# Moving the second half of the MLP's second product ahead of the second part of its first product

## The chip, the cores and the metric

The kernel runs on one core of a Trainium2 chip. The metric is the device time of one execution in microseconds. The kernel before took 2911.58 us, the median of three runs (2907.26 to 2915.17).

## The reference

Two stages follow one another. The first is a spectral layer over eight sequences of 3008 tokens and 256 channels; the second is an MLP over all 24064 tokens.

```python
X = np.fft.rfft(x, axis=1)
Yr = Xr @ w_r - Xi @ w_i + b_r
Yi = Xr @ w_i + Xi @ w_r + b_i
Yr = np.sign(Yr) * np.maximum(np.abs(Yr) - 0.01, 0.0)      # the same for Yi
x = np.fft.irfft(Yr + 1j * Yi, n=3008, axis=1)             # (8 * 3008, 256)
h = x @ w_in                                               # 256 -> 2048
g = np.maximum(0.01 * h, h)
out = g @ w_out                                            # 2048 -> 256
```

## The kernel before, in words

**Spectral part.** The transform of 3008 = 47 x 64 points is done in two stages of matmuls with constant matrices, per batch: `fwd` (fold, the transform over 47, `stage_a`), then `mid` (`stage_b`, the transform over 64; `proj`, the products with `w_r` and `w_i` and the soft threshold; `stage_g`, the way back over 64), then `inverse` (the way back over 47, at L480). Between these stages the data goes through DRAM (`u_dram`, `v_dram`). Their matmuls write PSUM banks of the tag `psf`, of which there are two. They are recorded at L78 (a helper that multiplies pairs), L343 and L480.

**MLP part.** The tokens are cut into 47 chunks of 512. In each chunk the 2048 hidden channels are cut into 8 groups of 256, so there are 47 x 8 = 376 steps `(ci, q)`. Every number is held as a high and a low part in fp32r, and a product is three matmuls (high by high, high by low, low by high).

For a step the first product (256 hidden channels by 512 tokens, over 256 channels) is cut into 2 x 2 blocks and made with seven block products instead of eight. `forms` (L496) makes the seven combinations of the tokens, `yh` and `yl`, once per chunk; those of the weights are made at the start.

- `moe_a` (L532, called part A here): four of the seven products, twelve matmuls of 256 columns at L92, into two PSUM banks `b1` and `b2` of the tag `psh` (four banks, so two steps). Then what was made is taken out: ACT copies the first half of `b1` (`p1`, L542), DVE adds the second half to it (`u2`, L543) and makes one of the four blocks of `g` (L545, L546).
- `moe_b` (L549, part B): the other three products, nine matmuls at L92, into the halves of the same two banks. So B's first product may only write once L542 and L543 have read, and its second once L546 has. Then ACT and DVE make the rest of `g`: the leaky ReLU of one block (L556), the sum of two blocks (L557), the leaky ReLU of three blocks (L559), the rounding to the high part `gh` (L561) and the low part `gl` (L563). `gf`, `gh` and `gl` have two buffers each.
- `moe_o` (L566, called with `eh` 0 or 1; parts O0 and O1): the second product for one half of the 256 output channels, two blocks of 128 hidden channels, six matmuls of 512 columns at L576, added up over the chunk's eight steps in a bank of the tag `pso`. It is that of two steps before (`LAG = 2`). After the chunk's last step ACT copies the bank (L581) and SP sends it out (L582).

**What sets the order.** `in_order` ties the matmuls of each part to the last matmul of the part before, in issue order only, so the parts' order on TensorE is that in which `moe` (L607) calls them:

```python
in_order(moe_a, ci, q)
if i >= LAG: in_order(moe_o, *steps[i - LAG], 0)
next(nxt, None); yield ...
in_order(moe_b, ci, q)
if i >= LAG: in_order(moe_o, *steps[i - LAG], 1)
next(nxt, None); ...; yield ...
```

At each `next(nxt, None)` a piece of the next chunk's `inverse` and `forms` is written down, at each `yield` a piece of the next batch's `fwd` and `mid`, as far as their shares are due. These are not tied: the framework's planner (`schedule_with_timeline_sim=True`) runs a timeline of its own over the whole program and puts each engine's instructions in the order in which they come to be ready there. The order so found is fixed in the program; on the chip each engine follows it and waits on semaphores.

Of the kernel before, what the change touches and what calls it, by code (L numbers as in the profile page):

```python
# [30 lines left out]
def spectral_mlp_kernel(  # L31
# [52 lines left out]
    def in_order(part, *args):  # L84

        with tc.issue_after(mlp[0].ins) if mlp else nullcontext():
            part(*args)
# [505 lines left out]
    def tokens(ci):  # L593

        yield
        for p in due[ci]:
            v_load(p)
            yield
        for _ in range(4 - len(due[ci])):
            yield  # L600
        for eh in range(NH):
            for p in due[ci]:
                inverse(p, eh)
                yield
        yield from forms(ci)

    def moe():  # L607

        for i, (ci, q) in enumerate(steps):
            if q == 0:  # L610
                nxt = tokens(ci + 1) if ci + 1 < nch else iter(())
            in_order(moe_a, ci, q)
            if i >= LAG:
                in_order(moe_o, *steps[i - LAG], 0)
            next(nxt, None)
            yield ci + (q + 0.5) / NQ
            in_order(moe_b, ci, q)
            if i >= LAG:
                in_order(moe_o, *steps[i - LAG], 1)
            next(nxt, None)  # L620
            if q == NQ - 1:
                for _ in nxt:
                    pass
            yield ci + (q + 1) / NQ
        for s in steps[-LAG:]:
            for eh in range(NH):
                in_order(moe_o, *s, eh)
# [92 lines left out]
    for i, pos in enumerate(moe()):  # L720
        if i % 2 == 0 and len(converted) < NQ:
            with tc.issue_after(made[0].ins):
                next(wout, None)
        if i in (2, 4):
            with tc.issue_after(parted[0].ins), tc.issue_after(parted[1].ins):
                next(fp.gen)
        while cur + 1 < NB - 1 and pos >= (read[cur + 1] if cur >= 0 else 0):
            for s in streams:
                s.finish()
            cur += 1  # L730
            streams = ([Stream(fwd(cur + 1), FWD + 4 * CS)] if cur else []) + [mids[cur]]
        frac = (pos - read[cur]) / (read[cur + 1] - read[cur]) if cur + 1 < NB else 1
        if cur == 0:
            frac = max(0, frac - 0.2) * 1.25
        work = frac / 0.95 * sum(s.total for s in streams)
        with tc.issue_after(converted[-1].ins) if cur == 0 else nullcontext():
            for s in streams:
                s.to(work / s.total)
                work = max(0, work - s.total)
# [103 lines left out]
```

## Time and profile before

| | |
|---|---|
| median of 3 runs | 2911.58 us (2907.26 to 2915.17) |
| the profiled execution | 2913.01 us, span 2911.2 us |
| TensorE (PE) busy | 2685.1 us, 92% of the span |
| VectorE (DVE) busy | 1896.7 us, 65% |
| ScalarE (ACT) busy | 1671.0 us, 57% |
| GpSimd (POOL) busy | 241.1 us, 8% |
| mean granted TensorE clock | 0.982 |
| first matmul of the MLP | 129.8 us after the start |

The times of rows are microseconds from the span's start and durations in microseconds; in groups the columns are the count, the busy time in us with the mean of one in ns, and the engine's idle time just before them in us with what ended it. PE rows are matmuls; their ends are modelled, and one starts while the one before still runs, so the distance from start to start says more than the duration. DVE and ACT rows are the instructions that read and write PSUM and SBUF.

### The profile page before, as it was taken

To read this page: it belongs to the slowest core of one execution; us is meant where nothing else is said; L and a number is where in the kernel's file an instruction comes from. 1 tells how busy PE (TensorE), PEld (TensorE's weight loads), DVE (VectorE), ACT (ScalarE), POOL (GpSimd) and SP (SyncE) were. 2 spreads that over 40 slices of the span, in tenths; PEclk is the share of its full clock that TensorE was granted. 3 is DMA by queue.
4 is the path that set the end of the run, shared out by engine and by line. 5 is a ranking of instruction groups with operands and counts; after the bars stand their busy time and mean duration, and the time that the engine had idled before them with its cause. 6 is when DMAs were issued, how large, how long until landed. Compare 5 with 4: busy or idle time off the path is not lost.

```text
span 2911.2 us, 43056 instructions
## 1 busy us (share of the span) xinstructions
PE 2685.1 (92%) x16300; PEld 2313.2 (79%) x16300; DVE 1896.7 (65%) x3403; ACT 1671.0 (57%) x3174; POOL 241.1 (8%) x180
## 2 busy tenths in 40 slices
PE   5989989999899999999999999999999999999988
PEld 4678878888788887888878887788887888777777
DVE  6676766666666666666666666666666766555554
ACT  4756645656565664566546665566655766454544
POOL 0001120001200012000110001100011000000000
PEclk8999999999999999999999999999999999999999
DMA  8521132111321113111222111221122111000000
GB/s 242 161 71 47 44 96 58 43 44 33 96 64 33 44 35 91 54 54 33 55 79 60 44 33 53 81 63 44 29 65 83 54 44 29 29 29 15 15 8 15
DMA packets 119916, 165.16 MB, mean 57 GB/s; under 512 B 13601, under 2 KB 69917, under 8 KB 119709
## 3 DMA queue, kind: packets, MB, share of 16 engines
q1 hardware_dynamic: 79120, 115.55, 13.0%
q10 hardware_dynamic: 40589, 46.87, 6.3%
q8 instruction: 128, 2.10, 0.3%
q14 instruction: 79, 0.65, 0.1%
HBM read 86.60 MB, written 75.76 MB: 56 GB/s over the span
## 4 chain that ended last, share of the span: by engine, by line
PE 43%; DVE 27%; ACT 18%; issue 4%; POOL 1%; DMA 1%; DVEq 0%; ACTq 0%; POOLq 0%; SPq 0%
PE psh L92 18%; PE pso L576 16%; DVE gl L563 7%; PE psf L78 7%; ACT gh L561 6%; ACT gf L559 5%; DVE gf L557 4%; DVE gf L545 3%; DVE gf L546 3%; DVE u L543 2%; PE psf L480 2%; PE psf L343 2%; ACT zf L400 1%; ACT zf L396 1%; DVE yl L506 1%
## 5 line engine op out<-in xcount | busy, mean ns | idle before, releaser
L92 PE MATMUL psh<-yh,win_hi 128*128 128x256 f32 x2632 | 792.3, 301 | 124.6 <-DVE gf L546 84.0
L563 DVE TENSOR_TENSOR gl<-gf,gh 128x1024 fp32r<-128x1024 f32 x376 | 466.1, 1240 | 448.7 <-ACT gh L561 444.4
L92 PE MATMUL psh<-yl,win_hi 128*128 128x256 f32 x2632 | 741.6, 282 | 0.1
L92 PE MATMUL psh<-yh,win_lo 128*128 128x256 f32 x2632 | 740.0, 281 | 0.0
L92 PEld LDWEIGHTS psh<-yh,win_hi 128*128 128x128 f32 x2632 | 500.4, 190 | 246.8 <-DVE gf L546 129.0
L576 PE MATMUL pso<-gh,wout_lo 128*128 128x512 f32 x1504 | 598.1, 398 | 0.0
L576 PE MATMUL pso<-gh,wout_hi 128*128 128x512 f32 x1504 | 598.0, 398 | 0.0
L576 PE MATMUL pso<-gl,wout_hi 128*128 128x512 f32 x1504 | 595.7, 396 | 0.0
L559 ACT ACTIVATE gf<-gf 128x768 f32<-128x768 f32 x376 | 318.3, 846 | 447.9 <-DVE gf L557 440.0
L92 PEld LDWEIGHTS psh<-yl,win_hi 128*128 128x128 f32 x2632 | 501.2, 190 | 23.3 <-DVE yl L506 0.3
L92 PEld LDWEIGHTS psh<-yh,win_lo 128*128 128x128 f32 x2632 | 500.1, 190 | 0.1
L561 ACT CAST gh<-gf 128x1024 fp32r<-128x1024 f32 x376 | 395.0, 1051 | 9.4 <-PE pso L576 3.2
L557 DVE TENSOR_TENSOR gf<-psh,u 128x512 f32<-128x512 f32 x376 | 258.4, 687 | 206.1 <-PE psh L92 205.7
L576 PEld LDWEIGHTS pso<-gl,wout_hi 128*128 128x128 f32 x1504 | 286.4, 190 | 65.6 <-DVE wout_lo L202 0.2
L576 PEld LDWEIGHTS pso<-gh,wout_hi 128*128 128x128 f32 x1504 | 287.0, 191 | 35.5 <-issue 0.2
L576 PEld LDWEIGHTS pso<-gh,wout_lo 128*128 128x128 f32 x1504 | 286.4, 190 | 32.1
L556 ACT ACTIVATE gf<-psh 128x256 f32<-128x256 f32 x376 | 145.2, 386 | 269.2 <-PE psh L92 248.6
L379 POOL TENSOR_TENSOR kb<-bias,kc 128x512 f32<-128x512 f32 x84 | 127.3, 1515 | 1714.0 <-ACT kc L376 1624.7
L543 DVE TENSOR_TENSOR u<-psh,p 128x256 f32<-128x256 f32 x376 | 157.1, 418 | 93.4 <-ACT p L542 93.3
L545 DVE TENSOR_TENSOR gf<-psh,u 128x256 f32<-128x256 f32 x376 | 158.7, 422 | 28.9 <-PE psf L78 0.5
L546 DVE TENSOR_TENSOR gf<-psh,gf 128x256 f32<-128x256 f32 x376 | 157.8, 420 | 6.1
L542 ACT COPY p<-psh 128x256 f32<-128x256 f32 x376 | 137.2, 365 | 16.2 <-PE psh L92 14.6
(134 smaller groups left out, 3274.7 us busy)
## 6 DMA issues: line engine op xcount, KB each, us to landing
u<-u_dram SPq DMA_DIRECT2D x192, 128.0 KB, 2.7
v_dram<-v ACTq DMA_DIRECT2D x192, 128.0 KB, 2.4
out_dram<-ob SPq DMA_DIRECT2D x94, 256.0 KB, 2.0
vin<-v_dram SPq DMA_DIRECT2D x96, 240.0 KB, 3.4
xin<-x_dram SPq DMA_DIRECT2D x90, 240.0 KB, 3.0
u_dram<-xin ACTq DMA_DIRECT2D x72, 240.0 KB, 2.4
u_dram<-xin SPq DMA_DIRECT2D x24, 240.0 KB, 4.0
raw<-w_out_dram SPq DMA_DIRECT2D x8, 512.0 KB, 5.1
```

What stands on the lines that cost most here:

```text
L78: last = nc.tensor.matmul(dst, a, b, start=(i == 0), stop=(i == len(terms) - 1))
L92: mlp[:] = [nc.tensor.matmul(dst, a, b, start=start and i == 0, stop=i == 2, skip_group_check=True)]
L542: act.copy(p1, b1[:, lo])
L543: dve.tensor_add(u2, b1[:, hi], p1)
L545: dve.tensor_add(g[:, 3], b2[:, hi], u2)
L546: dve.tensor_add(g[:, 3], b2[:, lo], g[:, 3])
L556: act.activation(g[:, 0], b1[:, lo], AF.Prelu, alpha=SLOPE)
L557: dve.tensor_add(g[:, 1:3], b2.rearrange("p (k n) -> p k n", k=2), u2.unsqueeze(1).broadcast_to([P, 2, HT]))
L559: act.activation(g[:, 1:4], g[:, 1:4], AF.Prelu, alpha=SLOPE)
L561: cp = act.copy(gh, g)
L563: parted[:] = [cp, dve.tensor_sub(gl, g, gh.bitcast(F32))]
L576: mlp[:] = [nc.tensor.matmul(po, a[:, f, s], r[:, i], start=(f == 0 and j == 0), stop=(f == NF - 1 and j == 2),)]
```

## The change

In `moe` the call of O1 goes from behind B to ahead of it. A step's order on TensorE was A, O0, B, O1; it is A, O0, O1, B. The piece of the next chunk (`next`) and the `yield` that stand between O0 and B now stand between O0 and O1. No instruction is added, removed or resized; the last `LAG` steps' O parts after the loop stay as they were.

```diff
@@ -614,9 +614,9 @@
                 in_order(moe_o, *steps[i - LAG], 0)
             next(nxt, None)
             yield ci + (q + 0.5) / NQ
-            in_order(moe_b, ci, q)
             if i >= LAG:
                 in_order(moe_o, *steps[i - LAG], 1)
+            in_order(moe_b, ci, q)
             next(nxt, None)
             if q == NQ - 1:
                 for _ in nxt:
```

## The prediction

> **What bounds the kernel now.** I read the first page for the shares, then the groups by line for what TensorE (PE) waits for, then the timeline of one step in the last chunks, where hardly any spectral work is left.
>
> ```profile
> span 2911.2 us, 43056 instructions
> PE 2685.1 (92%) x16300; PEld 2313.2 (79%) x16300; DVE 1896.7 (65%) x3403; ACT 1671.0 (57%) x3174; POOL 241.1 (8%) x180
> ```
> ```profile
> L92 PE MATMUL psh<-yh,win_hi 128*128 128x256 f32 x2632 | 792.3, 301 | 124.6 <-DVE gf L546 84.0 <-DVE u L543 39.3
> L576 PE MATMUL pso<-gh,wout_hi 128*128 128x512 f32 x1504 | 598.0, 398 | 0.0
> L78 PE MATMUL psf<-wr_hi,eh 128*128 128x256 f32 x336 | 79.4, 293 | 28.5 <-ACT eh L358 16.2 <-DVE yc L512 8.2 <-DVE eh L359 2.1
> L78 PE MATMUL psf<-xz,fa_hi 120*120 120x512 f32 (+1 forms) x168 | 62.9, 414 | 20.0 <-DVE xz L254 11.5 <-DVE xz L255 6.8 <-ACT gf L556 1.1
> L78 PE MATMUL psf<-zh,gb_hi 128*128 128x512 f32 x168 | 61.7, 426 | 9.8 <-ACT zh L407 5.8 <-ACT kc L376 3.2 <-DVE zh L408 0.2
> L480 PE MATMUL psf<-ga,vin 120*128 120x128 f32 x832 | 110.6, 276 | 2.4 <-DVE y L486 1.2 <-ACT v L418 0.3 <-ACT xin L264 0.3
> L343 PE MATMUL psf<-fb,u 128*128 128x128 f32 x672 | 89.0, 275 | 3.7 <-DMA u<-u_dram 1.8 <-ACT ob L581 0.9 <-ACT yc L493 0.6
> ```
> ```profile
> 0.00:130.00 130.00, 96.88 (x382) 65.82 (x383) 84.85 (x147) 77.80 (x151) 0.82 (x6) 0.88 0.71 209
> ```
>
> PE is the fullest engine. Its idle time is 2911.2 - 2685.1 = 226.1 us, and 124.6 us of it stand before the first matmul of an L92 product, nearly all for L546 and L543: the two vector instructions that empty the first product part's banks before the second part may write them. The first 130 us (set-up) hold 33.1 us of the idle time, so in the MLP stretch 124.6 of 193 us, 65%, is this one wait. Now one step of the last chunks, PE, then ACT, then DVE.
>
> ```profile
> 2823.72 0.39 PE L92 MATMUL psh<-yh,win_hi 128*128 128x256 f32 x1 [0.37 <-DVE gf L546]
> ...
> 2824.41 0.29 PE L92 MATMUL psh<-yh,win_lo 128*128 128x256 f32 x1
> 2824.54 0.39 PE L576 MATMUL pso<-gh,wout_hi 128*128 128x512 f32 x1
> 2824.77 0.40 PE L576 MATMUL pso<-gh,wout_lo 128*128 128x512 f32 x1
> 2825.93 0.28 PE L92 MATMUL psh<-yh,win_hi 128*128 128x256 f32 x1
> 2826.17 0.28 PE L92 MATMUL psh<-yh,win_lo 128*128 128x256 f32 x1
> 2826.28 0.28 PE L92 MATMUL psh<-yh,win_hi 128*128 128x256 f32 x1
> 2827.22 0.28 PE L92 MATMUL psh<-yh,win_lo 128*128 128x256 f32 x1
> 2827.34 0.40 PE L576 MATMUL pso<-gh,wout_hi 128*128 128x512 f32 x1
> 2828.48 0.39 PE L576 MATMUL pso<-gl,wout_hi 128*128 128x512 f32 x1
> 2829.05 0.38 PE L92 MATMUL psh<-yh,win_hi 128*128 128x256 f32 x1 [0.18 <-DVE u L543]
> 2830.03 0.38 PE L92 MATMUL psh<-yh,win_hi 128*128 128x256 f32 x1 [0.37 <-DVE gf L546]
> ```
> ```profile
> 2825.47 0.85 ACT L559 ACTIVATE gf<-gf 128x768 f32<-128x768 f32 x1 [1.70 <-DVE gf L557]
> 2826.35 1.05 ACT L561 CAST gh<-gf 128x1024 fp32r<-128x1024 f32 x1
> 2827.30 0.36 ACT L542 COPY p<-psh 128x256 f32<-128x256 f32 x1
> ```
> ```profile
> 2824.74 0.69 DVE L557 TENSOR_TENSOR gf<-psh,u 128x512 f32<-128x512 f32 x1 [1.08 <-PE psh L92]
> 2827.43 1.22 DVE L563 TENSOR_TENSOR gl<-gf,gh 128x1024 fp32r<-128x1024 f32 x1 [2.00 <-ACT gh L561]
> 2828.57 0.42 DVE L543 TENSOR_TENSOR u<-psh,p 128x256 f32<-128x256 f32 x1
> 2829.55 0.42 DVE L546 TENSOR_TENSOR gf<-psh,gf 128x256 f32<-128x256 f32 x1
> ```
>
> Call the parts A (first product, four products of three matmuls), B (three products) and O0, O1 (six matmuls each). Matmuls start 0.117 us apart at 256 columns (2826.17 to 2826.28 and the like) and 0.231 at 512 (2824.54 to 2824.77). The step repeats every 2830.03 - 2823.72 = 6.31 us, while its 21 + 12 matmuls need 21 x 0.117 + 12 x 0.231 = 5.23. The loop that takes 6.31 is not on PE: B's last matmul (2824.41) releases L557, then L559, L561, L563 follow one on the other; p of the next A, though its product was done at 2826.17 + 0.28 = 2826.45, runs behind L561 at 2827.30; u runs behind L563 at 2828.57; L546 ends at 2829.97 and lets B go on at 2830.03.
>
> **The floor.** For all matmuls at these distances: 376 steps x 5.23 = 1966 us. Spectral ones: the six groups of wr, wn, wd (336 with the high, 168 with the low part each), 1512 x 0.117 = 177; fa 252, of which by their two shapes 216 x 0.231 and 36 x 0.117 = 54; gb 252 x 0.231 = 58; ga and fb 1504 x 0.112 (estimate from eight of them in a row, below) = 168. With the 130 us ahead: 130 + 1966 + 457 = 2553 us. So PE starts are late by 358 us, more than the idle column shows, because a matmul's modelled end covers some of each gap. By the same 65%, 231 us belong to B's waits, 127 to spectral waits and ends.
>
> [...]
>
> **The change part by part.** Nothing is added or removed. Six matmuls a step, O1, go ahead of B. In the last step of a chunk's products the L581 copy and the output DMA of the second half go with them.
>
> Cover of A's emptying: PE runs O0 between A and B today, 6 x 0.231 = 1.39 us; afterwards O0 and O1, 2.77. Working the new step from the start of B's last matmul (t = 0) with the durations of the rows above: A follows at once, its four products are done at 0.63, 0.98, 1.33 and 1.68 (0.117 a start, 0.28 for the last one). L557 runs from 0.33 to 1.02; until then ACT has nothing, so p, which needs the first product only, fits in from 0.7 to 1.06, before L559. u runs from 1.1 to 1.5, L545 (0.42, the same shape) to 1.95, L546 to 2.4. PE reaches B at 0.12 + 12 x 0.117 + 2.77 = 4.3, so there are 1.9 us to spare. L563, not ready before 1.1 + 0.85 + 1.05 = 3.0, no longer gets between: the 1.22 us that stood before u come after L546. If p goes behind L559 instead, L546 ends at 3.3 to 3.6 and 0.7 us are still to spare. Gain where no spectral work is: 6.31 - 5.23 = 1.08 us a step.
>
> What is left of B's waits (231 us): lower end 0; upper end, if the emptying comes no sooner after A than now, what of each wait exceeds the added 1.39 us:
>
> ```profile
> PE psh L92 <- DVE gf L546: 84.0, 166, 3.2
> PE psf L78 <- ACT eh L358: 16.2, 10, 2.5
> ```
>
> In the first row (us in total, times, longest) the mean is 0.5 us and the longest wait 3.2, so about a third of the sum can stay, 70 us (an estimate). I take 35, nearer to none, since L563 is out of the way.
>
> The 127 us of spectral waits: from 0 to 127. Spectral matmuls keep the place ahead of B, but PE comes there with its queue full, so their inputs have had longer; on the other hand a step is shorter by 0.9. About half: 60.
>
> ```profile
> L581 ACT COPY ob<-pso 128x512 f32<-128x512 f32 x94 | 54.3, 577 | 58.5 <-PE pso L576 58.5
> ```
>
> Costed at nothing: O1's earlier place (gh and gl of two steps before were finished a step ago; the two buffers of each are read before B instead of after, so L561 finds them free sooner); the moved copies, 47 of the 94 in this row (ACT, which runs them, is 57% busy), and their 47 output DMAs on SP, which are now issued about one B ahead of where they were, before the loads that the planner's next steps put there; ACT and SP are behind PE here, as the row's 58.5 us of waiting for O shows, and cover gone, the copies would cost 47 x 0.58 = 27 us. At the end O0 of the last step has only the previous step's O parts ahead of it and waits some 1.2 us for L563.
>
> Sum: 2553 + 35 + 60 = 2648 of span. The profiled execution took 2913.0, 1.8 more than its span and 1.4 more than the median of 2911.6: 2650. Own range 2555 (nothing left) to 2752 (70 + 127).
>
> **Rivals.** *The emptying keeps its place.* The planner may leave p behind L561 and u behind L563. Then the loop from B's last matmul to the next B is what it was, and only O1 has changed sides: no change, 2912. Against it: in the step shown L561 began at 2826.35, 0.10 us before p's product was done, so the order there is that of readiness, and in the new step p is ready before L559. [...]
>
> *Spectral work falls behind.* Today a step has two openings for it, before B and between B's first two products:
>
> ```profile
> 1206.57 0.39 PE L78 MATMUL psf<-zh,gb_lo 128*128 128x512 f32 x1
> 1207.04 0.27 PE L92 MATMUL psh<-yh,win_lo 128*128 128x256 f32 x1
> 1207.15 0.28 PE L78 MATMUL psf<-wn_hi,eh 128*128 128x256 f32 x1
> 1208.45 0.28 PE L78 MATMUL psf<-wd_hi,eh 128*128 128x256 f32 x1
> 1213.44 1.05 PE L343 MATMUL psf<-fb,u 128*128 128x128 f32 x8
> ```
>
> With B ready early, both come at once, so a chain PE - ACT/DVE - PE gets one round a step. Needed: 672/8 = 84 frequency pairs at two rounds, 84 forward halves at one, 832/8 = 104 inverse halves two to a round: 304, against 312 steps before the last eight chunks. If a round takes 1.3 steps, 83 steps are missing; five are in hand, since the forms for a chunk are done long before it starts:
>
> ```profile
> 1490.25 0.68 DVE L506 TENSOR_TENSOR yl<-yc,yh 128x512 fp32r<-128x512 f32 x1
> 1527.30 0.28 PE L92 MATMUL psh<-yh,win_hi 128*128 128x256 f32 x1
> ```
>
> The other 78 would run with PE drained, each at up to the longest wait for such an input today, 2.5 us (the L358 row above): 195 us in place of the 60: 2785.
>
> *Slower.* If each of today's stretches needs a step of its own and nothing drains: the PE rows have 402 stretches of spectral matmuls, 145 of them inside B as shown; without the last chunks' about 380. With a step of 6.5 us (5.23 + 457/376, rounded up) and 5.35 in the last 64: 130 + 380 x 6.5 + 64 x 5.35 + 2 = 2944. It decides from about 376 such rounds on, where the same sum passes 2913. Against it: many stretches are two pieces of one round, and some steps have none.
>
> **How the numbers follow.** Forecast 0.65; spectral work behind 0.20; emptying in place 0.06; slower 0.07; something between, 0.02. A measurement of this kernel can tell about 0.3% from no change. Faster: 0.65 + 0.20 + the between and a part of the third: 0.89; same 0.04; slower 0.07. The range takes in most of the second case and of the forecast's own range: 2575 to 2800.
>
> **What would show it.** On ACT p ahead of L561, on DVE u and L546 ahead of L563; the L92 idle column from 124.6 to below 40; steps of 5.3 us in the last chunks and about 6.5 in the middle; POOL, DVE and ACT busy times unchanged. Wrong if PE waits at the first product of a chunk for L505/L506 (spectral work behind), if p still follows L561, or if the psf groups' idle time grows.

## The result and the profile after

The changed kernel takes 2604.09 us (median of 4 runs, 2600.34 to 2604.30) against 2909.90 (4 runs): a ratio of 0.8944, 95% interval 0.8928 to 0.8960. The prediction was 2650, with 2575 to 2800 as its range: faster, as forecast, and by 46 us more than forecast.

The first page and the PE groups of the profile after, in the columns used before:

```profile
span 2598.6 us, 42643 instructions
PE 2537.5 (98%) x16300; PEld 2281.5 (88%) x16300; DVE 1897.1 (73%) x3403; ACT 1668.5 (64%) x3174; POOL 229.6 (9%) x180
...
L92 PE MATMUL psh<-yh,win_hi 128*128 128x256 f32 x2632 | 752.3, 286 | 13.8 <-DVE gf L546 10.6 <-DVE u L543 3.0
L92 PE MATMUL psh<-yl,win_hi 128*128 128x256 f32 x2632 | 738.3, 280 | 0.6 <-DVE yl L506 0.5
...
L343 PE MATMUL psf<-fb,u 128*128 128x128 f32 x672 | 93.9, 275 | 9.6 <-DMA u<-u_dram 9.6
L78 PE MATMUL psf<-wr_hi,eh 128*128 128x256 f32 x336 | 77.9, 285 | 1.9 <-ACT eh L358 1.8
L78 PE MATMUL psf<-xz,fa_hi 120*120 120x512 f32 (+1 forms) x168 | 58.9, 380 | 0.0
L78 PE MATMUL psf<-zh,gb_hi 128*128 128x512 f32 x168 | 56.6, 396 | 0.0
```

ACT and DVE do the same work in the same time (DVE 1896.7 and 1897.1 us, ACT 1671.0 and 1668.5). What is gone is PE's waiting: 124.6 us before the products at L92 are 13.8, and the spectral groups, which waited 28.5, 20.0, 9.8 and 3.7 us, now wait 1.9, 0, 0 and 9.6. One of the last steps after, PE, then ACT, then DVE:

```profile
2525.17 0.28 PE L92 MATMUL psh<-yh,win_lo 128*128 128x256 f32 x1
2525.28 0.28 PE L92 MATMUL psh<-yh,win_hi 128*128 128x256 f32 x1
...
2525.87 0.28 PE L92 MATMUL psh<-yh,win_lo 128*128 128x256 f32 x1
...
2526.68 0.39 PE L576 MATMUL pso<-gh,wout_hi 128*128 128x512 f32 x1
...
2529.45 0.28 PE L92 MATMUL psh<-yh,win_hi 128*128 128x256 f32 x1
```
```profile
2526.18 0.37 ACT L542 COPY p<-psh 128x256 f32<-128x256 f32 x1 [1.27 <-PE psh L92]
2526.45 0.85 ACT L559 ACTIVATE gf<-gf 128x768 f32<-128x768 f32 x1
2527.34 1.06 ACT L561 CAST gh<-gf 128x1024 fp32r<-128x1024 f32 x1
```
```profile
2525.48 0.69 DVE L557 TENSOR_TENSOR gf<-psh,u 128x512 f32<-128x512 f32 x1
2526.59 0.42 DVE L543 TENSOR_TENSOR u<-psh,p 128x256 f32<-128x256 f32 x1 [0.41 <-ACT p L542]
2527.58 0.42 DVE L546 TENSOR_TENSOR gf<-psh,gf 128x256 f32<-128x256 f32 x1
2528.42 1.23 DVE L563 TENSOR_TENSOR gl<-gf,gh 128x1024 fp32r<-128x1024 f32 x1 [0.42 <-ACT gh L561]
```

B's last matmul starts at 2525.17, A at 2525.28. p now runs ahead of L559 and L561, u and L546 ahead of L563. L546 ends at 2528.00; B starts at 2529.45, and PE does not stop for it. Where the 312.6 us of span went, by stages (the view of busy time by stretch; columns: the stretch, its length, then busy time and count of PE, weight loads, DVE, ACT and POOL, granted clock, DMA), after and then before. The middle rows are the first 320 steps, the last rows the 56 steps that have little or no spectral work, with the end:

```profile
0.00:124.00 124.00, 93.25 (x381) 64.30 (x381) 84.62 (x147) 77.63 (x150) 0.82 (x6) 0.90 0.73 219
124.00:2286.50 2162.50, 2136.47 (x13971) 1940.59 (x13971) 1606.42 (x2903) 1416.94 (x2726) 228.73 (x174) 1.00 0.22 61
2286.50:2598.60 312.10, 307.74 (x1953) 276.59 (x1952) 206.02 (x354) 173.93 (x299) 0.00 (x0) 1.00 0.06 19
```
```profile
129.80:2537.50 2407.70, 2251.45 (x13972) 1968.82 (x13971) 1610.34 (x2904) 1420.43 (x2727) 240.27 (x174) 0.99 0.19 55
2537.50:2911.20 373.70, 336.94 (x1953) 278.79 (x1951) 201.51 (x352) 172.97 (x298) 0.00 (x0) 1.00 0.05 16
```

The middle gave 245.2 us, the last steps 61.6 (1.1 a step, the 1.08 of the prediction's clean step), the set-up 5.8.

### The profile page after: what moved, and what is told of

It reads as the page before. It is cut to its first block, busy times and chain, and to the rows that moved or that the text cites. A ratio compares the mean times of both kernels' runs of the same rounds, so it can differ in the third digit from the quotient of the medians.

```text
span 2598.6 us, 42643 instructions
## 1 busy us (share of the span) xinstructions
PE 2537.5 (98%) x16300; PEld 2281.5 (88%) x16300; DVE 1897.1 (73%) x3403; ACT 1668.5 (64%) x3174; POOL 229.6 (9%) x180
## 4 chain that ended last, share of the span: by engine, by line
PE 89%; DVE 3%; DMA 2%; ACT 1%; issue 0%; ACTq 0%; SPq 0%; DVEq 0%
PE pso L576 38%; PE psh L92 34%; PE psf L78 11%; PE psf L480 3%; PE psf L343 3%; DMA u<-u_dram 1%; DMA u_dram<-xin 1%; DVE yl L506 0%; DVE gl L563 0%; DMA raw<-w_out_dram 0%; DVE gf L557 0%; ACT gh L561 0%; DVE yt L511 0%; ACT gf L559 0%; DVE yc L512 0%
## 5 line engine op out<-in xcount | busy, mean ns | idle before, releaser
L92 PE MATMUL psh<-yh,win_hi 128*128 128x256 f32 x2632 | 752.3, 286 | 13.8 <-DVE gf L546 10.6
L92 PE MATMUL psh<-yl,win_hi 128*128 128x256 f32 x2632 | 738.3, 280 | 0.6 <-DVE yl L506 0.5
L92 PE MATMUL psh<-yh,win_lo 128*128 128x256 f32 x2632 | 737.9, 280 | 0.0
L576 PE MATMUL pso<-gh,wout_hi 128*128 128x512 f32 x1504 | 593.9, 395 | 0.0
L576 PE MATMUL pso<-gl,wout_hi 128*128 128x512 f32 x1504 | 591.1, 393 | 0.5 <-DVE gl L563 0.5
L576 PE MATMUL pso<-gh,wout_lo 128*128 128x512 f32 x1504 | 590.4, 393 | 0.0
L563 DVE TENSOR_TENSOR gl<-gf,gh 128x1024 fp32r<-128x1024 f32 x376 | 471.8, 1255 | 92.7 <-ACT gh L561 90.6
L92 PEld LDWEIGHTS psh<-yh,win_hi 128*128 128x128 f32 x2632 | 497.0, 189 | 30.7 <-DVE gf L546 15.4
L92 PEld LDWEIGHTS psh<-yl,win_hi 128*128 128x128 f32 x2632 | 497.0, 189 | 12.5 <-DVE yl L506 1.0
L92 PEld LDWEIGHTS psh<-yh,win_lo 128*128 128x128 f32 x2632 | 496.6, 189 | 0.2
L557 DVE TENSOR_TENSOR gf<-psh,u 128x512 f32<-128x512 f32 x376 | 259.1, 689 | 256.3 <-PE psh L92 255.1
L561 ACT CAST gh<-gf 128x1024 fp32r<-128x1024 f32 x376 | 396.4, 1054 | 7.1
L559 ACT ACTIVATE gf<-gf 128x768 f32<-128x768 f32 x376 | 320.0, 851 | 49.5 <-DVE gf L557 47.7
L576 PEld LDWEIGHTS pso<-gl,wout_hi 128*128 128x128 f32 x1504 | 282.5, 188 | 62.9 <-DVE gl L563 1.0
L576 PEld LDWEIGHTS pso<-gh,wout_hi 128*128 128x128 f32 x1504 | 283.1, 188 | 46.9 <-ACT gh L561 0.4
L576 PEld LDWEIGHTS pso<-gh,wout_lo 128*128 128x128 f32 x1504 | 282.9, 188 | 44.9
L379 POOL TENSOR_TENSOR kb<-bias,kc 128x512 f32<-128x512 f32 x84 | 119.0, 1417 | 1530.6 <-ACT kc L376 1409.6
L545 DVE TENSOR_TENSOR gf<-psh,u 128x256 f32<-128x256 f32 x376 | 159.3, 424 | 29.7 <-PE psh L92 2.0
L546 DVE TENSOR_TENSOR gf<-psh,gf 128x256 f32<-128x256 f32 x376 | 159.1, 423 | 9.0
```

What stands on the lines that cost most here:

```text
L92: mlp[:] = [nc.tensor.matmul(dst, a, b, start=start and i == 0, stop=i == 2, skip_group_check=True)]
L545: dve.tensor_add(g[:, 3], b2[:, hi], u2)
L546: dve.tensor_add(g[:, 3], b2[:, lo], g[:, 3])
L557: dve.tensor_add(g[:, 1:3], b2.rearrange("p (k n) -> p k n", k=2), u2.unsqueeze(1).broadcast_to([P, 2, HT]))
L559: act.activation(g[:, 1:4], g[:, 1:4], AF.Prelu, alpha=SLOPE)
L561: cp = act.copy(gh, g)
```

## The experiments

Two theories could explain such a gain. **Loop**: the limit was the loop B - L557 - L559 - gh (L561) - gl (L563) - u - L546 - B; the change breaks it because A is done sooner, so that the planner puts the emptying of A's banks (p, u, L545, L546) ahead of gh and gl in ACT's and DVE's queues. **Cover**: what counts is that PE has 1.39 us more work between A and B. The experiments set the two apart: the order on PE and the order in the queues are changed one without the other. All ratios are against the kernel before on the same chip (2907 to 2910 us). The diffs are shortened, and the comments in them are added. Where lines are added to a kernel, the line numbers below `moe_a` move by a few in its rows.

### The queue order alone (e1_late_cast)

```diff
+    def moe_c(ci, q, after=None):            # the end of moe_b, called one step later
+        g = cast_t.pop((ci, q))
...
+        with tc.issue_after(after[0].ins) ...: cp = act.copy(gh, g)              # behind p (L542)
...
+        with tc.issue_after(after[1].ins) ...: dve.tensor_sub(gl, g, gh...)      # behind L546
...
             in_order(moe_a, ci, q)
+            if i: moe_c(*steps[i - 1], emptied.pop((ci, q)))
```

> TensorE order of the kernel before (A, O0, B, O1), so the cover between A and B stays 1.39 us; only the queues differ: the cast to gh is issued behind the next step's p on ACT and gl behind the next step's L546 add on DVE. Loop theory (the limit was the loop B - L557 - L559 - gh - gl - u - L546 - B, broken when A's emptying goes ahead of gh and gl): from B's last matmul at 0, A starts at 1.5, p runs 2.05 to 2.4, the last add ends at 3.75, and PE gets to B at 4.3, so the wait is gone: steps of 5.3 to 5.5 us in the last chunks, total 2600 to 2690. Cover theory (what counts is the 1.39 us of matmuls more between A and B): no cover added, no gain: steps of 6.3 us, total 2880 to 2915.

2627.31 us, ratio 0.9036 (0.9022 to 0.9049); a step at the end, where there is no spectral work, takes 5.23 us (6.39 before; here and below the mean of the steps 370 to 373). On ACT and DVE the emptying is ahead of gh and gl in all 375 steps. The L92 row:

```profile
L92 PE MATMUL psh<-yh,win_hi 128*128 128x256 f32 x2632 | 756.1, 287 | 25.5 <-DVE gf L546 17.8 <-DVE u L543 7.0
```

With the order of the parts on PE untouched (the planner moved spectral matmuls among them), 281 of the 306 us come. The cover is not the main cause; whether it adds something is asked with e6.

### The cover without the queue order (e2_behind, e8_before_behind)

```diff
-        act.copy(p1, b1[:, lo])
-        dve.tensor_add(u2, b1[:, hi], p1)
+        with tc.issue_after(parted[0].ins) ...: act.copy(p1, b1[:, lo])              # behind gh
+        with tc.issue_after(parted[1].ins) ...: dve.tensor_add(u2, b1[:, hi], p1)    # behind gl
```

e2 makes this edit in the changed kernel, e8 in the kernel before.

> TensorE order of the changed kernel (A, O0, O1, B) with its 2.77 us of cover, but p is issued behind the gh cast of the step before and u behind its gl. Loop theory: gl ends at 4.2, u at 4.7, the last add at 5.5 after B's last matmul, PE is at B at 4.3, so the step is again 6.3 us in the last chunks and the total 2870 to 2930. Cover theory: the cover is what helps, total 2600 to 2690.

> The kernel before (A, O0, B, O1) with p behind the gh cast and u behind gl in all steps, where its planner does so in 240 of 375: the partner of e2, same queues, 1.39 us less cover. Loop theory: the loop does not go through O1, so the time is that of e2, 3000 to 3070. Cover theory: 1.39 us less cover in 376 steps should cost some 300 us against e2: 3250 to 3350.

e2: 3034.08 us, 1.0428 (1.0411 to 1.0446). e8: 3017.73 us, 1.0379 (1.0358 to 1.0400). A late step of e2, PE, ACT and DVE (there gh is L563, gl L565, u L545, the last add L548):

```profile
2991.94 0.28 PE L92 MATMUL psh<-yh,win_lo 128*128 128x256 f32 x1
2992.05 0.40 PE L578 MATMUL pso<-gh,wout_hi 128*128 128x512 f32 x1
...
2995.15 0.39 PE L92 MATMUL psh<-yh,win_hi 128*128 128x256 f32 x1 [0.20 <-DVE u L545]
...
2996.14 0.39 PE L92 MATMUL psh<-yh,win_hi 128*128 128x256 f32 x1 [0.37 <-DVE gf L548]
```
```profile
2992.45 1.05 ACT L563 CAST gh<-gf 128x1024 fp32r<-128x1024 f32 x1
2993.41 0.36 ACT L543 COPY p<-psh 128x256 f32<-128x256 f32 x1
```
```profile
2993.53 1.23 DVE L565 TENSOR_TENSOR gl<-gf,gh 128x1024 fp32r<-128x1024 f32 x1 [1.99 <-ACT gh L563]
2994.68 0.42 DVE L545 TENSOR_TENSOR u<-psh,p 128x256 f32<-128x256 f32 x1
2995.66 0.42 DVE L548 TENSOR_TENSOR gf<-psh,gf 128x256 f32<-128x256 f32 x1
```

A was done at 2992.2, p ran at 2993.41, u at 2994.68: with all the cover of the change, the step is 6.30 us again. With the queues fixed this way the 1.39 us are worth nothing (e2 is 16 us slower than e8). Both are above my 2870 to 2930 for e2, because I had equated them with the kernel before: its planner had put p ahead of gh in 135 of 375 steps, the edit in none, and that alone costs 110 us (e8). The late step was right, 6.30 us. e8, whose expectation followed e2's result, is in its range.

### Part of the cover, and none (e4_three, e5_no_cover, e7_nocover_late)

e4 moves three of O1's six matmuls; e5 and e7 call A, B, O0, O1, and e7 has e1's late cast besides.

```diff
+            if i >= LAG: in_order(moe_o, *steps[i - LAG], 1, 0, 3)     # e4: matmuls 0 to 2
             in_order(moe_b, ci, q)
+            if i >= LAG: in_order(moe_o, *steps[i - LAG], 1, 3, 6)     # e4: matmuls 3 to 5
```

> Only three of O1's six matmuls go ahead of B, three stay behind it: cover 2.08 us. Loop theory: p is ready 0.69 us sooner than in the kernel before, which is enough to be ahead of the gh cast; the planner now puts p ahead of gh in nearly all steps, but gl still between the last two adds in two steps of three, so a wait of some 0.3 us stays: steps of 5.3 to 5.7 us in the last chunks, total 2630 to 2720. Cover theory: half of the cover, half of the gain, steps of 5.85, total about 2755.

> Order A, B, O0, O1: nothing of the MLP between A and B, cover 0. Loop theory: the loop B - L557 - L559 - gh - gl - u - L546 - B is as long as in the kernel before, since A is done (4.5 us after B's last matmul) about when gl is (4.3): the last add ends at 5.5 to 5.7, steps of 6.2 to 6.5 us in the last chunks, total 2890 to 2970, hardly slower than before. Cover theory: each step loses the 1.39 us that covered the emptying: steps of 7.4 to 7.7, total above 3100.

> Order A, B, O0, O1 as in e5, but with gh and gl issued behind the next step's emptying as in e1. Loop theory, mended after e5 (there the gh cast also had to wait for O1 to release its buffer, and p and u stood behind it): with p and u free of the cast, A is done 4.5 us after B's last matmul, the last add at 5.1, so B's second product waits about 0.5 us and a step of the last chunks takes 5.7 to 6.0 us; total 2690 to 2800, faster than the kernel before without any MLP work between A and B. Cover theory: as e5, above 3100.

e4: 2650.48 us, 0.9113 (0.9094 to 0.9131), last steps 5.55 us. Half of the cover brings 258 of 306 us, inside the loop theory's range. With it the planner already puts p ahead of gh and u ahead of gl in 365 of 375 steps (135 before), though L546 ahead of gl only in 93. That this order brings the gain, and not the cover, is argued from e1 and e8; e4 changes both.

e5: 3297.55 us, 1.1337 (1.1315 to 1.1360), last steps 7.67. Here the loop theory's number failed and the cover theory's fitted, but a row of its waits (total, times, longest; 3.2 us in total before) shows why it does not decide between them:

```profile
ACT gh L561 <- PE pso L576: 303.0, 271, 2.8
```

With O0 and O1 behind B, the gh cast of this step waits for them to release its buffer (two buffers, the second product runs two steps late), and p stands behind the cast: the experiment had lengthened the loop by O0 and O1. e7 takes p and u out of it: 2842.71 us, 0.9777 (0.9757 to 0.9797). So with the right queue order the kernel is faster than before with no MLP work at all between A and B. The gain lies in the steps with spectral work: a late step takes 6.40 us, as long as before. The forecasts were 5.7 to 6.0 and 2690 to 2800, both missed; a late step shows by what:

```profile
2820.60 0.28 PE L92 MATMUL psh<-yh,win_hi 128*128 128x256 f32 x1
...
2821.19 0.28 PE L92 MATMUL psh<-yh,win_lo 128*128 128x256 f32 x1
...
2822.45 0.39 PE L92 MATMUL psh<-yh,win_hi 128*128 128x256 f32 x1 [0.28 <-DVE u L543]
...
2823.43 0.38 PE L92 MATMUL psh<-yh,win_hi 128*128 128x256 f32 x1 [0.36 <-DVE gf L546]
```
```profile
2821.56 0.37 ACT L542 COPY p<-psh 128x256 f32<-128x256 f32 x1 [1.93 <-PE psh L92]
```

p does not start when A's first product is done (2820.84 + 0.28 = 2821.12) but 0.44 us later, after the second one (2821.19 + 0.28 = 2821.47). In the changed kernel it is the same: A from 2525.28, p at 2526.18, the sixth matmul's end at 2526.15. Both products go to the same PSUM bank, and p waits for both: in none of the 376 steps of the twelve profiles does it start before the sixth matmul's end. Whether the chip or the framework ties p to the whole bank, no run here shows. With p 0.44 us sooner, e7's late step would take 5.96 us (an estimate from these rows), inside the forecast.

### One queue at a time (e11_gl_late, e12_gh_late)

The kernel before with only gl behind L546 (e11), and with only gh behind p (e12): each one of e1's two `issue_after`.

> The kernel before (A, O0, B, O1) with one queue changed: on DVE gl of a step is issued behind the next step's L546 add; ACT's order is left to the planner, which still puts p behind the gh cast in about half of the steps. Loop theory: with gl out of the way u needs only p, and even a p behind gh ends 2.9 to 3.3 us after B's last matmul, the last add at 4.7, against B at 4.3: most of the gain of e1, steps of 5.3 to 5.7 us in the last chunks, total 2630 to 2720. If p behind gh were the cause, little would change: 2850 to 2915.

> The kernel before with the other queue changed: on ACT the gh cast of a step is issued behind the next step's p; DVE's order is left to the planner, which now puts gl between the last two adds in 336 of 375 steps. Loop theory: gl (1.24 us) still stands in the loop, but only before the last add: gl ends at about 4.8 us after B's last matmul, the last add at 5.2, B's second product waits 0.5 us: steps of 5.6 to 6.0 us in the last chunks, total 2700 to 2790, about half of e1's gain. If p behind gh were the cause, it would be all of it: 2620 to 2640.

e11: 2680.49 us, 0.9209 (0.9182 to 0.9236), last steps 5.53. e12: 2781.43 us, 0.9556 (0.9528 to 0.9583), last steps 6.12. Three quarters of the gain (230 us) come with moving one vector instruction of 1.24 us out of the way, two fifths (129) with moving the cast alone. Neither is quite alone, since the planner answers in the other queue: in e11 p is ahead of gh in 181 steps (135 before), and in e12 u is ahead of gl in all 375, gl still ahead of the last add in 363. e12's late steps are a little longer than the 5.6 to 6.0 expected. The L92 rows of e11 and e12:

```profile
L92 PE MATMUL psh<-yh,win_hi 128*128 128x256 f32 x2632 | 766.5, 291 | 44.6 <-DVE gf L546 32.7 <-DVE u L543 11.3
L92 PE MATMUL psh<-yh,win_hi 128*128 128x256 f32 x2632 | 775.5, 295 | 101.8 <-DVE gf L546 95.1 <-DVE u L543 5.5
```

### Both together, and a try at what is left (e6_after_late, e9_mid_first)

e6 is the changed kernel with e1's edit. e9 is the changed kernel with this:

```diff
-            streams = ([Stream(fwd(cur + 1), FWD + 4 * CS)] if cur else []) + [mids[cur]]
+            streams = [mids[cur]] + ([Stream(fwd(cur + 2), FWD + 4 * CS)] if cur + 2 < NB else [])
```

> The changed kernel's TensorE order (A, O0, O1, B) and, as in e1, gh issued behind the next p and gl behind the next L546 in every step. Loop theory: in the changed kernel the planner already puts the emptying first in 311 of 375 steps, so forcing the rest takes away a part of the 13.8 us that the L92 products still wait: 2590 to 2610, no difference that matters. If the order of the queues and the cover each gave a part of their own, it would come out clearly below 2590.

> The changed kernel, with the spectral streams of each period in another order: first the middle stage of the batch whose forward stage is long done, then the forward stage of the batch after it, so that the first load of u does not follow the store to u_dram at once. In the changed kernel six waits of 1.3 to 2.6 us for that load, 10 us together, are the largest spectral wait left. If they go and nothing else moves: 2590 to 2597; if the first period, which now carries a forward stage more, gets too full: slower, 2610 to 2640.

e6: 2587.82 us, 0.8899 (0.8886 to 0.8912), the fastest kernel here and outside the changed kernel's interval. It fell 2 us below the range I gave for "no difference that matters", so that expectation missed by little. That the cover gives something of its own once the queues are in order shows against e1, which has the same queues and 1.39 us less cover: 40 us. A late step is 5.23 us in both, so these lie in the steps with spectral work. e6's L92 row and the set of medians:

```profile
L92 PE MATMUL psh<-yh,win_hi 128*128 128x256 f32 x2632 | 747.9, 284 | 9.2 <-DVE gf L546 5.8 <-DVE u L543 3.2
```

| us | emptying behind gh and gl | as the planner puts it | emptying ahead |
|---|---|---|---|
| A, B, O0, O1 (cover 0) | - | 3298 (behind in 372 of 375) | 2843 |
| A, O0, B, O1 (1.39) | 3018 | 2908 | 2627 |
| A, O0, O1, B (2.77) | 3034 | 2604 | 2588 |

With the emptying ahead, the first 1.39 us of cover are worth 215 us and the next 1.39 are worth 40; with it behind, the next 1.39 are worth nothing.

e9: 2617.11 us, 0.9003 (0.8988 to 0.9018), slower than the changed kernel. The wait for u that it was to remove is still there, 10.0 us against 9.6, because the edit does not part the store from the load. The streams still follow one another as `mid` of batch 1, `fwd` of 2, `mid` of 2, `fwd` of 3 and so on; only the period in which a `fwd` falls has changed. First e9's wait (total, times, longest), the last store of batch 2 (issued by ACT), the loads (issued by SP) and the matmul that waits; then the same rows of the changed kernel:

```profile
PE psf L343 <- DMA u<-u_dram: 10.0, 5, 5.3
420.87 0.32 ACTq L267 DMA_DIRECT2D u_dram<-xin  x1
421.17 7.87 SPq L329 DMA_DIRECT2D u<-u_dram  x8
425.73 2.05 PE L343 MATMUL psf<-fb,u 128*128 128x128 f32 x8 [5.30 <-DMA u<-u_dram]
```
```profile
436.18 10.01 SPq L329 DMA_DIRECT2D u<-u_dram  x8
437.80 0.32 ACTq L267 DMA_DIRECT2D u_dram<-xin  x1
443.80 1.13 PE L343 MATMUL psf<-fb,u 128*128 128x128 f32 x8 [2.29 <-DMA u<-u_dram]
```

So e9 says nothing against the store, and the traces speak for it. In the changed kernel this store lands at 440.90, the third load is issued at 440.91 and lands at 443.66, and PE goes on at 443.80. In e6 the third load is issued just as soon after the store has landed (443.50 and 443.48), but PE has other matmuls until then: past the set-up it waits for no load of u. That is part of the 16 us by which e6 is faster than the changed kernel.

The stretch of e9 shows the forecast's other branch: in the period that carries one more forward stage, PE is idle for 16.3 of 90 us, 5.3 of them in the wait just shown. Below it, the changed kernel in the same stretch:

```profile
350.00:440.00 90.00, 73.69 (x401) 62.27 (x399) 57.77 (x101) 42.98 (x81) 18.97 (x15) 0.87 0.34 95
```
```profile
350.00:440.00 90.00, 90.00 (x560) 80.26 (x559) 68.81 (x118) 53.57 (x94) 18.90 (x14) 1.00 0.34 97
```

## Why the prediction was right, point by point

**The bound.** It named the loop through L557, L559, L561, L563, u and L546 and not PE or any engine's load. e1, e11, e2 and e8 show it: the place of gh and gl decides most of it, and the cover adds 40 us where that place is right.

**The emptying moves ahead.** The planner did so: in 332 of 375 steps p is ahead of L559, and in 313 L546 is ahead of gl (counted in the ACT and DVE rows; 9 and 18 before, where gl was ahead of u in 240). The step that p "needs the first product only" was wrong: it waits for both products of the bank. So the emptying ends 2.8 us after B's last matmul and not 2.4, and PE has 1.45 us to spare and not 1.9. It did not matter here; e7 missed by it. By the same error, p in the step shown before was ready at 2826.8, 0.45 us after L561 began, not 0.10, and waited 0.5 us behind it, not the 0.85 from 2826.45 to 2827.30. In the late step of e2, where p is issued behind gh, ACT kept that order: p's bank was done at about 2991.5 (A's sixth matmul, 2991.24 + 0.28), gh began at 2992.45, and p ran at 2993.41, behind it.

**The floor.** 2553 us, of which 2423 after the set-up, held: with the set-up of 124.0 the floor of this run is 2547, and its span 2598.6 is 52 us above it, where the prediction had 95. The forecast of about 6.5 us for a middle step spread the spectral work over all 376 steps; nearly all of it lies in the first 320, which makes 5.23 + 457/320 = 6.66, and they take 6.76 (2162.5/320).

**The remaining waits.** Too large, both. Of the 30.4 us of PE idle time past the set-up (2598.6 - 124.0 - 2537.5 + 93.3), 13.8 stand before L92; at the same share of the 52 us, B's waits are 23 (35 forecast) and the rest 28 (60 forecast). The largest single item of the rest, and the one spectral wait that grew (3.7 to 9.6 us), is the way of u through DRAM shown with e9. With the set-up's 6 us, which nothing in the change accounts for (in e6 the first product comes at 129.4 again), these terms make up the 49 us between 2648 and 2598.6.

**Spectral work.** The step that failed is in the second rival: "With B ready early, both come at once, so a chain PE - ACT/DVE - PE gets one round a step." The spectral work got more openings, not fewer: in PE's order there are 630 stretches of spectral matmuls in place of 419 (402 of these in the prediction's two openings), and 312 of them lie in places that had next to none, within A, within and between the O parts, and between B and A. With PE seldom held up before B, they slip in where they become ready. e2 fits this: with the same order of the parts, but PE held up, there are 369 stretches, 351 of them ahead of B or between its first two products. What the planner weighs is argued from this, not shown. The rival's other sign is there in small: the forms of a chunk are done some 20 us ahead of it and not 35, and in the one chunk past the set-up where they are late PE waits 0.5 us for L506.

**The rivals.** Emptying in place did not occur, and was priced wrongly at "no change": e2 puts it at 3034, because the kernel before was already a mixture of both orders. The slower case (one round a step for every stretch) had the false premise just named.

## What to carry to other kernels

When PE waits for two short instructions that empty a bank, look at what stands in front of them in their queue before adding work to cover them: here one vector instruction of 1.24 us in the wrong place was worth 230 us, and 1.39 us of added cover nothing while the queues stood in the wrong order. A change of order on one engine can work through the order that a planner then gives to another; compare all queues, and pin the order that matters (e6). Before reading an experiment, look in its trace whether the edit did what it was meant to (e9). An edit that removes cover may also lengthen a buffer's life (e5), so read the new waits before taking it as a test of the cover.

## What the runs showed of the hardware

The granted clock did not fall when PE became fuller. It is 0.993 at 98% busy, 0.982 at the 92% of the kernel before, and lowest in e5, where PE is busy for 85%; the mean granted clock of the changed kernel, then of e5:

```profile
core 0: 2598.6 us, clock 0.993
```
```profile
core 0: 3297.8 us, clock 0.956
```

A mean matmul at L576 of the first kind (`wout_hi` with `gh`) takes 395 ns in the changed kernel and 415 in e5. What sets the granted clock, no run here shows.
